# Where the top-32 mask of an attention block is made: VectorE's masked multiply, or a steep Prelu and an Exp with row sums on ScalarE

## The chip, the cores and the metric

The kernel runs on one core of a Trainium2 chip. The core has five engines, each with an instruction queue of its own that runs strictly in order: TensorE (PE, with its weight loads shown apart as PEld), VectorE (DVE), ScalarE (ACT), GpSimd (POOL) and SyncE (SP, which here only issues DMAs). They wait for each other through semaphores. The metric is the device time of one launch in microseconds (us); lower is better.

## The reference, cut to what matters

Attention that keeps the 32 largest scores of each row, followed by two feed-forward blocks.

```python
scores = scale * np.matmul(q, k.transpose(0, 1, 3, 2))     # 4 batches, 8 heads, 576 x 576, scale 1/8
kth = np.partition(scores, -32, axis=-1)[..., -32:-31]
scores = np.where(scores >= kth, scores, -1e9)
attn = np.exp(scores - max(scores)); attn /= attn.sum(-1) + 1e-9
x = attn @ v
h = x @ w_in;  g = P(h) / (Q(h) + 1e-6);  y = g @ w_out    # 2304 tokens, 512 -> 2048 -> 512
h = y @ w_in2; g = h * np.cos(h);         out = g @ w_out2
```

## The kernel before

**Attention.** A unit is 128 query rows of one pair of heads, so a tile of scores is 128 x 2 x 576 in fp32, and there are 72 units. `qk(i)` multiplies on PE into the PSUM tile `sx`, and ACT copies each head's half (j = 0, 1) into the SBUF tile `sS`. `topk(i)` is a generator of pieces. DVE takes the larger and the smaller of the two half rows into `e` (two TENSOR_TENSOR), and then finds the 32 largest in four rounds of MAX8 with MATCH_REPLACE8 between them; they end up sorted in `hd`, so `hd[0]` is the row's maximum and `hd[31]` the threshold. ACT makes `nb`, the maximum times -1/8, after the first round. After the last round ACT writes exp(score/8 + nb) for the whole row over `e`. Then, in two last pieces (one for each j), DVE reads `sS` and `e` once more: it keeps `e` where the score is at least the threshold, writes zero elsewhere, and adds up the row into `sum`. That is the SCALAR_TENSOR_TENSOR `e<-sS,hd,e`, and its row sum comes out with a DVE_READ_ACCUMULATOR. `av(i)` transposes `e` on PE (`pp`), ACT copies the transposes to SBUF (`pt`), and PE multiplies by v. `norm` divides by the row sums.

**Feed-forward blocks.** Eight units make 256 tokens, and for these the two blocks run in 8 groups each: `in1`, `mid1`, `end1`, `out1`, then `in2`, `mul2`, `out2`. Every fp32 product is three fp32r matmuls (high and low parts). ACT evacuates PSUM (`w`, `hs`) and does Abs, Ln, Exp, Sin and the affine steps; DVE and POOL do the products of two tensors.

**Weights.** In the first 16 units or so the kernel also takes 64 pieces of 64-bit weights apart into fp32 high and low parts (`conv`, tiles `raw`, `cb`), on ACT, POOL, DVE and PE, and stores low parts back to DRAM.

**Order.** The pieces of `topk` and the steps of the feed-forward blocks are laid into one list of slots, five slots to a unit. The mask pieces of unit i run in the first slot of unit i + 1, ahead of `av(i)`. From there a scheduler that follows the list and a modelled timeline settles the order on each engine's queue. `sS` and `e` have two buffers each. All ACT, DVE and POOL instructions are recorded by one helper, so they all show line L79.

Of the kernel before, what the change touches and what calls it, by code (L numbers as in the profile page):

```python
# [10 lines left out]
F32 = mybir.dt.float32  # L11
# [3 lines left out]
AF = mybir.ActivationFunctionType  # L15
ALU = mybir.AluOpType
# [7 lines left out]
P = 128  # L24
# [3 lines left out]
SCALE = 0.125  # L28
HALF = S // 2
NEG = -3.0e38  # L30
VW = 640
TWO_PI = 6.283185307179586
MAGIC = 12582912.0
# [16 lines left out]
NC0 = 36  # L50
C2 = 80
PM = 150
PMASK = range(0)
WA, PA = 12, 90
WG, PG = 10, 90
N1, NU, N2, NST, NGG = 2, 2, 3, 4, 3
# [32 lines left out]
def body(tc, out, qt, kt, vt, ident_d, w1_d, w1o_d, a_d, b_d, w2_d, w2o_d):  # L89
    nc = tc.nc  # L90
    V, A, G = Windowed(tc, nc.vector, WIN, PM), Windowed(tc, nc.scalar, WA, PA), Windowed(tc, nc.gpsimd, WG, PG)
    PE, SP = nc.tensor, nc.sync

    with ExitStack() as ctx:
        def pool(name, bufs=1, **k):
            return ctx.enter_context(tc.tile_pool(name=name, bufs=bufs, **k))
# [5 lines left out]
        sml = pool("sml", 4)  # L102
# [25 lines left out]
        sx = ps_s.tile([P, 2, 512], F32, name="sx")  # L128
# [6 lines left out]
        def store_k(x, b, pr):  # L135
            raw, hi = x[:, 0].bitcast(F32), x[:, 1]
            A.activation(hi, raw, AF.Copy)
            G.tensor_sub(raw, raw, hi.bitcast(F32))
            hi = hi.bitcast(F32)
            top, bot = slice(0, D), slice(D, P)  # L140
            d = kdr[b, pr]
            for o, i_ in ((d[top, 0], hi[top]), (d[bot, 0], raw[top]), (d[bot, 1], hi[bot]), (d[top, 1], raw[bot])):
                SP.dma_start(out=o, in_=i_)
# [36 lines left out]
        def load_v(i):  # L180
# [4 lines left out]
            for j, (b, _) in enumerate(qts[n]):  # L185
                v = kv.tile([P, VW], F32, tag="v", bufs=VB, name=f"v{i}_{b}")
                A.dma_start(out=v, in_=vt[b, pr])
# [91 lines left out]
        def halves(ap):  # L279
            return ap.rearrange("p (a c) -> p a c", a=2)  # L280

        def after(mm, bank):
            for x in order[bank]:
                tc.add_manual_dep(mm.ins, x, mybir.DependencyInfo(mybir.DependencyClass.NoSync, mybir.DependencyReason.DATA), reason="bank")

        def qk(i):
            n, pr = units[i]
            raw, hi, lo = (*qpair[i // 2], None, None)[:3]
            kvs = ins[i]
            m = P // len(kvs)  # L290
            st[i] = sb = att.tile([P, 2, S], F32, tag="sS", bufs=2, name=f"sS{i}")
            for j in range(2):
                rows = slice(j * D, (j + 1) * D)
                for c, (k, _) in reversed(list(enumerate(kvs))):
                    q0 = i % 2 * P
                    qs, qc = slice(0, (c + 1) * m), slice(q0, q0 + (c + 1) * m)
                    for hf in range(2):
                        o = sx[qs, hf, :HALF]
                        hs = slice(hf * HALF, (hf + 1) * HALF)
                        if n < 2:  # L300
                            mm = PE.matmul(o, raw[rows, j, qc], k[rows, 0, hs].bitcast(F32), start=True, stop=True)
                            after(mm, hf)
                        else:
                            mm = PE.matmul(o, hi[:, j, qc], k[:, j, hs], start=True, stop=False, skip_group_check=True)
                            after(mm, hf)
                            mm = PE.matmul(o, lo[:, j, qc], k[:, j, hs], start=False, stop=True, skip_group_check=True)
                        order[hf] = [mm.ins.name]
                A.activation(halves(sb[:, j]), sx[:, :, :HALF], AF.Copy)
            if n == 1:
                store_k(kvs[0][0], 0, pr)  # L310

        def topk(i):
            n, pr = units[i]
            sc = st.pop(i)
            tiles = [sc[:, j] for j in range(2)]
            e = att.tile([P, 2, S], F32, tag="e", bufs=EB, name=f"e{i}")
            et[i] = e
            kb, t = n // 2, n % 2
            if i % 8 == 0:
                sums[kb] = sml.tile([P, 2, H], F32, tag="sum", bufs=2, name=f"sum{kb}")  # L320
            sm = sums[kb][:, t]
            hds = sml.tile([P, 2, 32], F32, tag="hd", bufs=2, name=f"hd_{i}")
            hd = [hds[:, j] for j in range(2)]
            nb = sml.tile([P, 2], F32, tag="nb", bufs=2, name=f"nb_{i}")
            big = [e[:, j, :HALF] for j in range(2)]
            both = [e[:, j] for j in range(2)]

            def top(j, x, r):
                V.max(out=hd[j][:, 8 * r:8 * r + 8], in_=x[j])

            def drop(j, x, r):
                V.match_replace(out=x[j], in_to_replace=hd[j][:, 8 * r:8 * r + 8], in_values=x[j], imm_value=NEG)

            l, r = sc[:, :, :HALF], sc[:, :, HALF:]
            V.tensor_tensor(e[:, :, :HALF], l, r, op=ALU.max)
            top(0, big, 0)
            yield
            V.tensor_tensor(e[:, :, HALF:], l, r, op=ALU.min)
            top(1, big, 0)
            A.activation(nb, hds[:, :, 0], AF.Copy, scale=-SCALE)  # L340
            yield
            for step in (((drop, big, 0), (top, big, 1)), ((drop, big, 1), (top, both, 2)), ((drop, both, 2),)):
                for f, *x in step:
                    for j in range(2):
                        f(j, *x)
                yield
            for j, s in enumerate(tiles):
                top(j, both, 3)
                A.activation(e[:, j], s, AF.Exp, bias=nb[:, j:j + 1], scale=SCALE)
            yield  # L350
            for j, s in enumerate(tiles):
                row = sm[:, 2 * pr + j:2 * pr + j + 1]
                if i in PMASK:
                    G.tensor_scalar(s, s, hd[j][:, 31:32], 1.0, op0=ALU.is_ge, op1=ALU.mult)
                    G.tensor_mul(e[:, j], e[:, j], s)
                    A.activation(s, e[:, j], AF.Copy, accum_out=row)
                else:
                    V.scalar_tensor_tensor(e[:, j], s, hd[j][:, 31:32], e[:, j], op0=ALU.is_ge, op1=ALU.mult, accum_out=row)
                yield

        def av(i):
# [279 lines left out]
        def attention():  # L641
            load_k(1)
            load_v(0)
            qk(0)
            prev = None
            nrm, fresh, held = [], [], []
            for i in range(nu + 1):
                if LQ == 0 and i % 2 == 0 and i + 2 < nu:
                    load_q(i + 2)
                if i + 1 < nu:  # L650
                    qk(i + 1)
                if i + 2 < nu:
                    load_k(i + 2)
                for x, a in held:
                    store_k(x, *a)
                held = [(prep(*a), a) for a in preps.get(i, [])]
                t = topk(i) if i < nu else iter([None] * 9)
                for p in range(5):
                    if p == 0 and prev is not None:
# [49 lines left out]
def _layout(q, k, v, moe_w_in, moe_w_out, moe_a, moe_b, moe2_w_in, moe2_w_out):  # L709
# [9 lines left out]
    vp = v.reshape(B, NP, 2, S, D)  # L719
    vh = np.zeros((B, NP, P, VW), np.float32)  # L720
    vh[..., :512] = vp[:, :, :, :512].reshape(B, NP, 2, 4, P, D).transpose(0, 1, 4, 3, 2, 5).reshape(B, NP, P, 512)
# [19 lines left out]
```

## Time and profile before

| | |
|---|---|
| time, median of 3 runs | 1469.39 us (1466.33 to 1470.24) |
| the profiled execution | 1473.49 us, its span 1471.7 us |
| PE busy | 1270.3 us, 86% of the span |
| DVE busy | 1283.4 us, 87% |
| ACT busy | 1082.1 us, 74% |
| POOL busy | 680.4 us, 46% |
| mean granted TensorE clock | 0.92 |
| bytes moved by DMA | 314.98 MB, mean 214 GB/s |

Busy time is the time in which at least one instruction of the engine is under way. Instructions overlap a little at their ends, and matmuls a good deal, so the mean duration of one is longer than its share of the queue. The shares of the whole span mix stages: the attention pieces run from the start to about 1277 us, the weights are taken apart until about 356 us, and after 1277 us only feed-forward work is left.

### The profile page before, as it was taken

The page shows a single profiled execution, that of the slowest core. Times are in us where ns is not written, and L with a number is a line of the kernel's source. Part 1 is how long each engine was busy: PE and PEld are TensorE (multiplying, and loading weights), DVE is VectorE, ACT ScalarE, POOL GpSimd, SP SyncE. Part 2 cuts the span into 40 slices and gives each one's busy share as a digit, 9 for nine tenths or more (in the row PEclk, how much of TensorE's full clock was granted, in tenths as well). Part 3 has the DMA queues.
Part 4 walks back from the last instruction along what each step waited for, and adds up shares of the span by engine and source line. Part 5 has one row for each costly group of instructions (what it writes and reads, how often), then busy time and mean ns, then how long its engine had stood idle before and what let it go on. Part 6 is the DMA issues. An engine that isn't in the chain of part 4 may idle for free.

```text
span 1471.7 us, 25059 instructions
## 1 busy us (share of the span) xinstructions
PE 1270.3 (86%) x9016; PEld 1120.9 (76%) x9016; DVE 1283.4 (87%) x2477; ACT 1082.1 (74%) x1873; POOL 680.4 (46%) x503
## 2 busy tenths in 40 slices
PE   5766787657898799989988998999999899999988
PEld 2434565546896698889888997888899799988986
DVE  6999999789999999989989999999999999745533
ACT  5777778665787678778877877878878577876643
POOL 3879466654354346335544644444545344420000
PEclk9677798757999899999999999999999999999999
DMA  7886756775456656555765665565467677656677
GB/s 227 286 280 209 238 183 201 239 229 197 136 190 200 208 183 211 190 175 205 241 221 176 219 212 190 182 215 198 176 219 247 215 253 260 226 196 226 233 239 230
DMA packets 141549, 314.98 MB, mean 214 GB/s; under 512 B 12016, under 2 KB 28528, under 8 KB 141424
## 3 DMA queue, kind: packets, MB, share of 16 engines
q1 hardware_dynamic: 122832, 261.99, 53.4%
q10 hardware_dynamic: 18592, 51.39, 10.4%
q8 instruction: 71, 1.16, 0.3%
q14 instruction: 54, 0.44, 0.1%
HBM read 278.20 MB, written 35.13 MB: 213 GB/s over the span
## 4 chain that ended last, share of the span: by engine, by line
DVE 37%; PE 28%; ACT 13%; DMA 11%; issue 6%; POOL 5%; SPq 0%; ACTq 0%; POOLq 0%; DVEq 0%
DVE e L79 17%; DVE hd L79 8%; PE o L558 6%; DVE u L79 5%; PE h L444 4%; PE h L446 4%; PE h L445 4%; DVE cb L79 2%; POOL cb L79 2%; PE y L503 2%; PE y L502 2%; ACT L79 2%; DMA raw<-w 2%; DMA w1ol<-w1ol 2%; PE y L501 2%
## 5 line engine op out<-in xcount | busy, mean ns | idle before, releaser
L79 DVE MAX8 hd<-e 128x8 f32<-128x288 f32 (+1 forms) x576 | 322.3, 592 | 0.0
L558 PE MATMUL o<-w2o,gg 128*128 128x512 f32 x864 | 233.8, 409 | 9.7 <-DMA w2o<-w2o 8.5
L79 DVE MATCH_REPLACE8 e<-hd,e 128x288 f32<-128x288 f32 (+1 forms) x432 | 230.2, 537 | 0.0
L558 PEld LDWEIGHTS o<-w2o,gg 128*128 128x128 f32 x864 | 160.6, 197 | 40.5 <-DMA w2o<-w2o 9.9
L79 DVE TENSOR_TENSOR e<-sS 128x576 f32<-128x576 f32 x144 | 166.9, 1196 | 24.9 <-ACT sS L79 15.2
L444 PE MATMUL h<-xh,w1hi 128*128 128x256 f32 x576 | 171.6, 298 | 12.5 <-ACT hs L79 6.3
L502 PE MATMUL y<-gg,w1o 128*128 128x256 f32 x576 | 169.3, 294 | 6.7 <-POOL gg L79 6.6
L445 PE MATMUL h<-xl,w1hi 128*128 128x256 f32 x576 | 167.6, 291 | 6.8 <-DVE xl L79 6.8
L501 PE MATMUL y<-gg,w1o 128*128 128x256 f32 x576 | 169.2, 294 | 4.6 <-ACT gg L79 4.6
L79 POOL TENSOR_TENSOR gg<-u,gg 128x512 fp32r<-128x512 f32 x64 | 91.8, 1435 | 174.5 <-ACT gg L79 158.8
L444 PE MATMUL h<-x2h,w2hi 128*128 128x256 f32 x576 | 165.9, 288 | 5.2 <-ACT w L79 2.7
L503 PE MATMUL y<-gg,w1ol 128*128 128x256 f32 x576 | 167.8, 291 | 1.6 <-DMA w1ol<-w1ol 1.5
L446 PE MATMUL h<-x2h,lo 128*128 128x256 f32 x576 | 164.9, 286 | 3.2 <-DMA lo<-w2lo 3.2
L446 PE MATMUL h<-xh,lo 128*128 128x256 f32 x576 | 166.4, 289 | 0.0
L445 PE MATMUL h<-x2l,w2hi 128*128 128x256 f32 x576 | 164.5, 286 | 2.1 <-DVE x2l L79 2.1
L79 DVE SCALAR_TENSOR_TENSOR e<-sS,hd,e 128x576 f32<-128x576 f32 x144 | 151.7, 1068 | 16.4 <-ACT e L79 16.2
L79 POOL TENSOR_TENSOR u<-u,w 128x512 f32<-128x512 f32 x64 | 91.8, 1435 | 157.3 <-ACT u L79 148.9
L79 POOL TENSOR_TENSOR rr<-rr,hs 128x512 f32<-128x512 f32 x56 | 78.2, 1418 | 127.7 <-ACT rr L79 127.7
L79 ACT ACTIVATE e<-sS,nb 128x576 f32<-128x576 f32 x144 | 107.9, 772 | 29.8 <-DVE hd L79 29.5
L444 PEld LDWEIGHTS h<-xh,w1hi 128*128 128x128 f32 x576 | 113.4, 197 | 18.1 <-ACT hs L79 8.4
L502 PEld LDWEIGHTS y<-gg,w1o 128*128 128x128 f32 x576 | 113.9, 198 | 10.9 <-POOL gg L79 9.0
L501 PEld LDWEIGHTS y<-gg,w1o 128*128 128x128 f32 x576 | 114.3, 198 | 9.1 <-ACT gg L79 7.5
(1167 smaller groups left out, 3793.1 us busy)
## 6 DMA issues: line engine op xcount, KB each, us to landing
w2o<-w2o SPq DMA_DIRECT2D x144, 512.0 KB, 4.2
lo<-w1lo SPq DMA_DIRECT2D x72, 512.0 KB, 4.0
w1ol<-w1ol SPq DMA_DIRECT2D x72, 512.0 KB, 3.8
lo<-w2lo SPq DMA_DIRECT2D x72, 512.0 KB, 4.4
k<-kdr ACTq DMA_DIRECT2D x44, 576.0 KB, 5.0
raw<-w SPq DMA_DIRECT2D x32, 512.0 KB, 4.6
v<-vt ACTq DMA_DIRECT2D x48, 320.0 KB, 3.7
qr<-qt ACTq DMA_DIRECT2D x36, 256.0 KB, 4.0
```

The source lines that it names most:

```text
L79: r = f(*a, **k)
L444: PE.matmul(h[:, i, :], wh, xh[:, c, :], start=(c == 0), stop=False)
L445: PE.matmul(h[:, i, :], wh, xl[:, c, :], start=False, stop=False)
L446: PE.matmul(h[:, i, :], lo[:, i, c, :], xh[:, c, :], start=False, stop=(c == NCC - 1))
L501: PE.matmul(y[:, c, :], w1o[:, f, cs], gh[:, i, :], start=(f == 0 and c % 2 == 0), stop=False, skip_group_check=True)
L502: PE.matmul(y[:, c, :], w1o[:, f, cs], gl[:, i, :], start=False, stop=False, skip_group_check=True)
L503: PE.matmul(y[:, c, :], wl[:, i, cs], gh[:, i, :], start=False, stop=(f == NF - 1), skip_group_check=True)
L558: PE.matmul(o[:, t, :], l[:, i, ts], wt[i][:, r], start=(f == 0 and r == 0 and l is gh), stop=(f == NF - 1 and l is gl), skip_group_check= ...
```

## The change

The scores are scaled by 1/8 as they leave PSUM. After the last MAX8, ACT makes `nt` = -threshold for both heads. For each head it writes Prelu(score - threshold) over `e`, with slope 1 above zero and 2^120 below, then makes `nb` = threshold - maximum with an Identity, and then writes Exp(e + nb) in place, with the row sum in the same instruction. What lies under the threshold has become hugely negative, so its exponential is zero. The mask pass on DVE is gone, and with it the early `nb`.

```diff
+STEEP = 2.0 ** 120
...
-                A.activation(halves(sb[:, j]), sx[:, :, :HALF], AF.Copy)
+                A.activation(halves(sb[:, j]), sx[:, :, :HALF], AF.Copy, scale=SCALE)
...
             nb = sml.tile([P, 2], F32, tag="nb", bufs=2, name=f"nb_{i}")
+            nt = sml.tile([P, 2], F32, tag="nt", bufs=2, name=f"nt_{i}")
...
             top(1, big, 0)
-            A.activation(nb, hds[:, :, 0], AF.Copy, scale=-SCALE)
             yield
...
-            for j, s in enumerate(tiles):
+            for j in range(2):
                 top(j, both, 3)
-                A.activation(e[:, j], s, AF.Exp, bias=nb[:, j:j + 1], scale=SCALE)
             yield
-            for j, s in enumerate(tiles):
-                row = sm[:, 2 * pr + j:2 * pr + j + 1]
...
-                    V.scalar_tensor_tensor(e[:, j], s, hd[j][:, 31:32], e[:, j], op0=ALU.is_ge, op1=ALU.mult, accum_out=row)
+            for j in range(2):
+                if j == 0:
+                    A.activation(nt, hds[:, :, 31], AF.Copy, scale=-1.0)
+                A.activation(e[:, j], sc[:, j], AF.Prelu, bias=nt[:, j:j + 1], alpha=STEEP)
+                A.activation(nb[:, j:j + 1], hd[j][:, 0:1], AF.Identity, scale=-1.0, bias=hd[j][:, 31:32])
+                A.activation(e[:, j], e[:, j], AF.Exp, bias=nb[:, j:j + 1], accum_out=sm[:, 2 * pr + j:2 * pr + j + 1])
                 yield
```

ACT's queue before, between two evacuations of unit 36's transposes, with the exponentials of unit 37 (`e37`; `h`, `w`, `r`, `rr`, `n`, `gg`, `ob` belong to the feed-forward blocks):

```order
L79 ACTIVATE pt36a_6564<-pp36a_6559 128x512
L79 ACTIVATE sS38_6537<-sx_94 128x576
L79 ACTIVATE e37_6549<-sS37_6326,nb_37_6551 128x576 x2
L79 ACTIVATE hs2_2_6703<-h1_2_2_6677 128x512
L79 ACTIVATE r3_4_6623<-q3_4_6622,qc_114 128x512
L79 ACTIVATE rr2_2_6702<-hs2_2_6703,quarter_110 128x512
L79 ACTIVATE pt36b_6571<-pp36b_6566 128x512
```

Both exponentials of unit 37 stand side by side, right behind an evacuation of scores. ACT's queue now, at the same place:

```order
L79 ACTIVATE pt36a_6675<-pp36a_6670 128x512
L79 ACTIVATE n2_2_6816<-rr2_2_6813,magic_112 128x512
L79 ACTIVATE nb_37_6660<-hd_37_6659 128x1
L79 ACTIVATE nt_37_6661<-hd_37_6659 128x2
L79 ACTIVATE nb_37_6660<-hd_37_6659 128x1
L79 ACTIVATE e37_6658<-sS37_6429,nt_37_6661 128x576 x2
L79 ACTIVATE w3_5_6938<-h0_3_5_6913 128x512
L79 ACTIVATE e37_6658,sum4_5631<-e37_6658,nb_37_6660 128x576
L79 ACTIVATE ob1_0_6836<-o1_5408 128x512
L79 ACTIVATE sS38_6643<-sx_94 128x576
L79 ACTIVATE gg1_3_4_6983<-u3_4_6735 128x512
L79 ACTIVATE e37_6658,sum4_5631<-e37_6658,nb_37_6660 128x576
```

The three small instructions and both Prelus stand where the two exponentials stood; the exponentials follow with other work between them. In both programs the whole ACT queue holds 67 ACT_TABLE_LOADs.

DVE's queue before, from unit 37's last rounds to unit 38's first:

```order
L79 MATCH_REPLACE e37_6549<-hd_37_6550,e37_6549 128x576 x2
L79 MAX hd_37_6550<-e37_6549 128x8 x2
L79 SCALAR_TENSOR_TENSOR u3_4_6624<-u3_4_6624,nega_108,w3_4_6621 128x512
L79 SCALAR_TENSOR_TENSOR e37_6549,sum4_5537<-sS37_6326,hd_37_6550,e37_6549 128x576 x2
L79 SCALAR_TENSOR_TENSOR q3_4_6622<-q3_4_6622,r3_4_6623 128x512
L79 SCALAR_TENSOR_TENSOR u3_4_6624<-u3_4_6624,nega_108,r3_4_6623 128x512
L79 SCALAR_TENSOR_TENSOR rr2_2_6702<-n2_2_6705,rr2_2_6702 128x512
L79 SCALAR_TENSOR_TENSOR u3_4_6624<-q3_4_6622,u3_4_6624 128x512
L79 TENSOR_TENSOR e38_6749<-sS38_6537 128x2x288 x2
```

The masks of unit 37 (`e37_6549,sum4_5537`) stand between steps of `end1`. DVE's queue now, at the same place:

```order
L79 MATCH_REPLACE e37_6658<-hd_37_6659,e37_6658 128x576 x2
L79 MAX hd_37_6659<-e37_6658 128x8 x2
L79 SCALAR_TENSOR_TENSOR q3_4_6733<-q3_4_6733,r3_4_6734 128x512
L79 SCALAR_TENSOR_TENSOR u3_4_6735<-u3_4_6735,nega_108,r3_4_6734 128x512
L79 SCALAR_TENSOR_TENSOR rr2_2_6813<-n2_2_6816,rr2_2_6813 128x512
L79 SCALAR_TENSOR_TENSOR u3_4_6735<-q3_4_6733,u3_4_6735 128x512
L79 TENSOR_TENSOR e38_6861<-sS38_6643 128x2x288 x2
```

The two mask instructions, which waited for ACT's exponentials, are gone from between the last MAX8 and the next unit.

## Rows read from the trace of the kernel before

**Rows 1.** Busy time of each engine by stage: us, busy (instructions), clock, DMA, GB/s

```profile
core 0: us, PE busy (x) PEld busy (x) DVE busy (x) ACT busy (x) POOL busy (x), PEclk, DMA share, GB/s
...
29.00:166.00 137.00, 92.97 (x353) 54.97 (x354) 133.88 (x254) 100.62 (x194) 108.16 (x87) 0.69 0.78 255
166.00:356.00 190.00, 131.03 (x745) 105.74 (x744) 169.92 (x289) 131.95 (x242) 111.57 (x88) 0.76 0.68 219
356.00:485.00 129.00, 108.97 (x854) 99.56 (x851) 125.90 (x261) 96.95 (x169) 61.09 (x42) 0.97 0.54 176
485.00:1161.00 676.00, 630.29 (x4832) 583.30 (x4832) 642.09 (x1299) 533.33 (x925) 325.43 (x225) 0.97 0.60 204
1161.00:1277.00 116.00, 113.41 (x981) 106.96 (x983) 109.01 (x212) 89.32 (x153) 48.44 (x35) 0.97 0.70 242
1277.00:1471.70 194.70, 179.71 (x1239) 163.81 (x1235) 87.34 (x136) 114.19 (x165) 16.52 (x13) 0.99 0.68 225
```

**Rows 2.** The page's chain that ended last: its share of the span by engine

```profile
DVE 37%; PE 28%; ACT 13%; DMA 11%; issue 6%; POOL 5%; SPq 0%; ACTq 0%; POOLq 0%; DVEq 0%
```

**Rows 3.** Groups of the whole run: count, busy us, mean ns, idle before and releaser

```profile
L79 DVE SCALAR_TENSOR_TENSOR e<-sS,hd,e 128x576 f32<-128x576 f32 x144 | 151.7, 1068 | 16.4 <-ACT e L79 16.2
L79 DVE DVE_READ_ACCUMULATOR e<-sS,hd,e 128x1 f32 x144 | 11.1, 77 | 0.0
L79 ACT ACT_TABLE_LOAD x67 | 86.0, 1283 | 3.4 <-issue 2.1
```

**Rows 4.** The mask pass in two stretches, 29 to 166 us, then 485 to 1161 us

```profile
L79 DVE SCALAR_TENSOR_TENSOR e<-sS,hd,e 128x576 f32<-128x576 f32 x17 | 22.6, 1333 | 1.2 <-ACT e L79 1.2
...
L79 DVE SCALAR_TENSOR_TENSOR e<-sS,hd,e 128x576 f32<-128x576 f32 x81 | 79.8, 1004 | 9.5 <-ACT e L79 9.3
```

**Rows 5.** ACT's groups from 485 to 1161 us

```profile
L79 ACT ACTIVATE e<-sS,nb 128x576 f32<-128x576 f32 x80 | 59.5, 771 | 14.1 <-DVE hd L79 14.0
...
L79 ACT ACTIVATE n<-rr,magic 128x512 f32<-128x512 f32 x40 | 28.7, 717 | 1.2 <-DMA out<-ob 0.8
L79 ACT ACTIVATE r<-w 128x512 f32<-128x512 f32 x40 | 25.2, 630 | 1.5 <-POOL gg L79 1.0
...
L79 ACT ACTIVATE nb<-hd 128x2 f32<-128x2 f32 x40 | 8.1, 201 | 28.3 <-DVE hd L79 28.0
```

**Rows 6.** ACT's timeline at four places: start us, duration us, instruction

```profile
685.00 0.20 ACT L79 ACTIVATE nb<-hd 128x2 f32<-128x2 f32 x1 [1.48 <-DVE hd L79]
685.11 0.71 ACT L79 ACTIVATE n<-rr,magic 128x512 f32<-128x512 f32 x1
...
695.09 1.45 ACT L79 ACTIVATE e<-sS,nb 128x576 f32<-128x576 f32 x2
696.43 0.60 ACT L79 ACTIVATE hs<-h 128x512 f32<-128x512 f32 x1
...
697.52 0.72 ACT L79 ACTIVATE rr<-hs,quarter 128x512 f32<-128x512 f32 x1
698.14 0.60 ACT L79 ACTIVATE pt36b<-pp36b 128x512 f32<-128x512 f32 x1
...
1302.62 0.71 ACT L79 ACTIVATE rr<-hs,quarter 128x512 f32<-128x512 f32 x1
1303.37 0.72 ACT L79 ACTIVATE n<-rr,magic 128x512 f32<-128x512 f32 x1
```

**Rows 7.** Waits of ACT, then of DVE, 485 to 1161 us: total, times, longest

```profile
ACT nb L79 <- DVE hd L79: 28.0, 24, 2.6
...
ACT e L79 <- DVE hd L79: 14.0, 15, 2.5
...
DVE e L79 <- ACT e L79: 9.3, 7, 2.5
```

**Rows 8.** Waits of all engines, 166 to 356 us: total, times, longest

```profile
ACT raw L79 <- DMA raw<-w2o: 12.3, 9, 4.3
...
PE pp13a L374 <- DVE e L79: 9.1, 1, 9.1
```

More of the change, by code (lines that the diff above doesn't have):

```diff
@@ L52 @@
 PM = 150
-PMASK = range(0)
 WA, PA = 12, 90
@@ L314, in topk @@
             sc = st.pop(i)
-            tiles = [sc[:, j] for j in range(2)]
             e = att.tile([P, 2, S], F32, tag="e", bufs=EB, name=f"e{i}")
@@ L346, in topk @@
                 yield
-            for j, s in enumerate(tiles):
+            for j in range(2):
                 top(j, both, 3)
-                A.activation(e[:, j], s, AF.Exp, bias=nb[:, j:j + 1], scale=SCALE)
             yield
-            for j, s in enumerate(tiles):
-                row = sm[:, 2 * pr + j:2 * pr + j + 1]
[L353 to L357, printed above, removed]
-                    V.scalar_tensor_tensor(e[:, j], s, hd[j][:, 31:32], e[:, j], op0=ALU.is_ge, op1=ALU.mult, accum_out=row)
+            for j in range(2):
[4 more added lines that the diff above has]
+                A.activation(e[:, j], e[:, j], AF.Exp, bias=nb[:, j:j + 1], accum_out=sm[:, 2 * pr + j:2 * pr + j + 1])
                 yield
```

## The prediction

> **What bounds the kernel now.** I read busy time by stage first, because the shares of the whole span mix stages with different limits [rows 1]. I cut at the first transposes of units 0, 8, 16, 24, 64 and 71. Eight units take 137 us, then 190, then 129; the forty units from 485 to 1161 us take 676, about 135 for eight; the last seven take 116; and 194.7 us of feed-forward work are left when the attention pieces are over. The reader is to see which engine is fullest in each. DVE is busy 133.88 of 137 us, 169.92 of 190, 125.90 of 129 and 642.09 of 676: 98, 89, 98 and 95%. From 1161 us on it is PE, 113.41 of 116 (98%). PE stands close behind DVE in the long stretch too, 630.29 of 676 (93%), but matmuls overlap, so this count holds the time in which a matmul drains while nothing follows it. ACT has 533.33 of 676 (79%). Then the chain of waits: DVE has 37% of it, PE 28%, ACT 13%, DMA 11% [rows 2]. So DVE leads until 1161 us, but not alone. Work that leaves DVE is worth something until then, and nothing after.
>
> **The change part by part.**
>
> *Removed from DVE.* 144 mask passes, 151.7 us in all, 1068 ns each; the 144 reads of the accumulator (77 ns) lie inside the start of the next instruction [rows 3]. An instruction overlaps its neighbour by about 0.07 us, so some 1.0 us of queue goes with each, 2.0 us per unit. By stage: 22.6 us from 29 to 166 us, where one pass takes 1333 ns, and 79.8 us from 485 to 1161 us [rows 4]; in the two stages between, 16 passes of 1.0 us each. DVE's wait for ACT's exponential ahead of the mask goes too, 9.3 us in the long stretch [rows 7].
>
> *Added to ACT.* Per unit, two Prelus over 576 elements and one small instruction for each head; `nt` takes the place of the old `nb`, the same shape, at no change. The trace has no Prelu; the nearest row is the exponential, the same tile with the same kind of bias operand, 771 ns alone [rows 5], and two of them hold the queue for 1.34 us before the next starts [rows 6]. So 0.67 us each. The small `nb` now takes a bias from memory: the old one holds the queue 0.11 us [rows 6], and a bias operand adds 717 - 630 = 87 ns, by two operations of one shape with and without it [rows 5]. So 0.20 us each. The row sum out of the exponential has no row on ACT. From below it costs nothing, as DVE's read does; from above, as much as a small instruction, 0.20 us. I take 0.08, DVE's duration, which is the nearest row. Last, an instruction that reads what the one right ahead of it wrote: Identity to Identity starts 0.75 us after when it depends and 0.62 when it doesn't [rows 6], so 0.13 us. The order above puts other work between most of them; I take one per unit. The sum is 2 x 0.67 + 2 x 0.20 + 2 x 0.08 + 0.13 = 2.0 us per unit. The ends are 2 x 0.67 + 2 x 0.11 = 1.6, and 2 x 0.77 + 2 x 0.30 + 2 x 0.20 + 4 x 0.13 = 3.1 us.
>
> *Is a pass on ACT dearer than on DVE?* Over the same 128 x 576 fp32 the exponential takes 771 ns and the mask 1068 [rows 3, 5]. The Trainium skill, ScalarE: Activation LUTs, Rules for kernel authors, says the opposite: simple steps such as relu, max and mul belong on VectorE, which it puts at up to about three times faster per element in bf16. By that rule a Prelu would cost ACT more than the 1068 ns that DVE gives up; the trace shows the reverse for this fp32 pass.
>
> *Moved and free.* The scale on the copy out of PSUM replaces a constant; nothing is added. The new program holds as many table loads as the trace of before, 67 at 1283 ns [rows 3], so Prelu brings no switch. The early `nb` had ACT wait 28.0 us for the first MAX8 in the long stretch, and the exponential another 14.0 for the last [rows 7]; now there is one such wait, on the last MAX8. Behind it on ACT's queue stand an evacuation of `h` and one of scores, and PE and DVE wait for these, as they did behind the exponential. `e` now comes from ACT, at the end of a row of dependent instructions, instead of from DVE. The order leaves several ACT instructions between the second exponential and the first evacuated transpose that needs it, so I cost this at nothing; if that cover goes, PE waits by its transposes. The worst such wait of before is 9.1 us, once [rows 8]. The 8 x 2.0 us per group of units on DVE and the same on ACT nearly cancel; what counts is that DVE was at 95 to 98% and ACT at 79.
>
> **The sum by stage.** I allow the fullest engine 95%, what DVE holds in the long stretch.
> - 29 to 166 us: DVE falls to 112, ACT rises to 100.6 + 16 = 117, POOL has 108. 117 / 0.95 = 123; with three engines so near each other I take 126: **-11**.
> - 166 to 356 us: DVE 153, ACT 148, PE 131 at a granted clock of 0.76. DVE's 20 us of idle time are where the weights' DMAs set the pace (ACT waits 12.3 us for `raw` [rows 8]). If all of the removed work counts it is -18, if the DMAs hold it 0; I take half: **-9**.
> - 356 to 485 us: DVE 110, ACT 113, PE 109. 113 / 0.95 = 119: **-9**.
> - 485 to 1161 us: DVE 642 - 75 = 567, ACT 533 + 81 = 614, PE 630. ACT at 95% gives 646, PE at the 98% that it reaches after 1161 us gives 643. I take 650: **-26**.
> - 1161 to 1277 us: PE is at 98% already: **-1**. After that nothing changes.
>
> That is -56, so the profiled execution would go from 1473.5 to about 1418. It stood 4.1 us above the median of 1469.4; taken off, **1414 us**.
>
> **The rivals.**
> - *PE and the handoffs hold the long stretch.* PE's 93%, and its 28% of the chain, speak for it; that DVE has the larger share of the chain speaks against. Then only the first three stages gain, 29 us: **1440 us**.
> - *ACT takes DVE's place, and it is slower.* At 3.1 us per unit ACT gets 533 + 124 = 657 in the long stretch; at 95% that is 692, 16 us more than now. The first and third stages give 132 and 128 (-5 and -1), the last one of the attention +1. Sum +11: **1480 us**. The point from which it decides is 0.95 x 676 - 533 = 109 us on forty units, 2.7 us per unit. For it: the row sum's price is unknown, and every evacuation that PE needs stands in the same queue. Against: four of its prices would all have to be at their upper ends.
> - *More than I take.* With 1.6 us per unit ACT has 597 in the long stretch, 628 at 95% (-48), PE's count shrinks as its waits do, and the three stages before it give their full -18, -18 and -13: -97, **1372 us**. PE's 630 speaks against it.
> - *The wait only moves.* ACT waits for the last MAX8 and everyone behind it waits along, as much as DVE saves: **1468 us**. The waits that go, 28.0 and 9.3 us, speak against.
>
> **How the numbers follow.** My forecast 0.50, with a range of its own of 1390 to 1432; PE holds it 0.20; more 0.10; no change 0.06; slower 0.14. A measurement of this kernel can't tell less than about 0.3%, some 4 us, from no change. So faster 0.80, same 0.06, slower 0.14. The range leaves out the slower case and half of the case with more, and takes in no change: 1372 to 1468.
>
> **What would show it right or wrong.** In the profile after, no SCALAR_TENSOR_TENSOR on `e`, and DVE's busy time near 1135 us; ACT's near 1082 + 145 = 1227; Prelu near 0.77 us; the stage of forty units at about 650 us with ACT at 95%. If ACT's groups on `e` and `nb` add up to over 2.7 us per unit more than before, the slower case is on. If DVE falls and the long stretch keeps its 676 us, PE's waits will say who holds it: waits for `w`, `hs` or `pt` from ACT mean the queue there, none mean PE itself. I would be wrong at the root if the transposes of `e` waited on ACT in every unit.

## The result: 1.2% slower, and the profile after

The changed kernel takes 1485.86 us (median of four runs, 1484.74 to 1494.18) against 1467.89 us before (four runs); the ratio is 1.0116, with a 95% interval of 1.0079 to 1.0153. The forecast was 1414 us, faster. The profiled execution after is 1494.18 us, its span 1492.4 us; it is the longest of the four, 8.3 us above their median, so its stages are a little long.

The first part of the page of the changed kernel, busy time over the whole run:

```profile
PE 1274.8 (85%) x9016; PEld 1122.6 (75%) x9016; DVE 1145.2 (77%) x2189; ACT 1200.6 (80%) x2305; POOL 667.5 (45%) x503
```

DVE has lost 138 us (1283.4 before; 148 were forecast) and ACT gained 118.5 (1082.1 before; 145 were forecast). The time went the other way all the same. Busy time by stage, cut at the same units as [rows 1] (us; busy time and count of each engine, granted clock, share of DMA, GB/s):

```profile
27.00:165.00 138.00, 92.35 (x355) 54.17 (x353) 117.91 (x221) 115.30 (x245) 105.31 (x88) 0.70 0.80 257
165.00:347.00 182.00, 122.41 (x699) 97.66 (x699) 148.04 (x250) 139.74 (x282) 106.08 (x86) 0.77 0.67 217
347.00:485.00 138.00, 118.75 (x896) 109.00 (x895) 122.55 (x240) 114.02 (x227) 62.28 (x43) 0.94 0.54 174
485.00:1184.00 699.00, 641.61 (x4855) 591.05 (x4856) 565.59 (x1136) 602.41 (x1167) 320.23 (x225) 0.96 0.60 198
1184.00:1304.00 120.00, 116.69 (x1026) 109.49 (x1025) 89.41 (x180) 102.40 (x197) 51.03 (x37) 1.00 0.73 247
1304.00:1492.40 188.40, 169.99 (x1170) 154.71 (x1168) 87.44 (x137) 110.34 (x163) 14.43 (x11) 0.98 0.69 221
```

The long stretch of forty units has gone from 676 to 699 us, and in it no engine is full any more: DVE is at 81%, ACT at 86%, and PE's count at 92%, below its 93% of before. The first and third stages have not gained either (137 to 138, 129 to 138); the second has (190 to 182), and so has the feed-forward work at the end, which the change does not touch (194.7 to 188.4). PE's own busy time in the long stretch is 11.3 us more than before (630.29 to 641.61), at a mean granted clock of 0.96 instead of 0.97.

The new instructions on ACT, in its groups of the whole run (count, busy us, mean ns, idle us before, releaser):

```profile
L79 ACT ACTIVATE e<-e,nb 128x576 f32<-128x576 f32 x144 | 110.5, 770 | 0.2
L79 ACT ACTIVATE e<-sS,nt 128x576 f32<-128x576 f32 x144 | 103.5, 767 | 0.0
...
L79 ACT ACTIVATE nb<-hd 128x1 f32<-128x1 f32 x144 | 41.3, 288 | 22.6 <-DVE hd L79 22.5
...
L79 ACT ACTIVATION_READ_ACCUMULATOR e<-e,nb 128x1 f32 x144 | 28.0, 195 | 0.0
```

The places where other engines stand idle, in the page's groups, of the changed kernel first and then of the kernel before:

```profile
L79 DVE TENSOR_TENSOR e<-sS 128x576 f32<-128x576 f32 x144 | 159.7, 1148 | 124.8 <-ACT sS L79 71.5
...
L440 PE MATMUL h<-xh,w1hi 128*128 128x256 f32 x576 | 173.7, 302 | 23.0 <-ACT hs L79 10.0
...
L497 PE MATMUL y<-gg,w1o 128*128 128x256 f32 x576 | 169.8, 295 | 13.9 <-ACT gg L79 13.9
L440 PE MATMUL h<-x2h,w2hi 128*128 128x256 f32 x576 | 167.4, 291 | 10.8 <-ACT w L79 9.9
```

```profile
L79 DVE TENSOR_TENSOR e<-sS 128x576 f32<-128x576 f32 x144 | 166.9, 1196 | 24.9 <-ACT sS L79 15.2
L444 PE MATMUL h<-xh,w1hi 128*128 128x256 f32 x576 | 171.6, 298 | 12.5 <-ACT hs L79 6.3
...
L501 PE MATMUL y<-gg,w1o 128*128 128x256 f32 x576 | 169.2, 294 | 4.6 <-ACT gg L79 4.6
...
L444 PE MATMUL h<-x2h,w2hi 128*128 128x256 f32 x576 | 165.9, 288 | 5.2 <-ACT w L79 2.7
```

The first DVE instruction of a unit, the TENSOR_TENSOR on the scores, had 24.9 us of idle time ahead of it before and has 124.8 now, 71.5 of it for ACT's copy of the scores out of PSUM. Not all of this is the work of the new instructions: `x1_no_mask` below, which takes the mask off DVE and adds nothing to ACT, already has 86.3 us there, and is fast.

```profile
L79 DVE TENSOR_TENSOR e<-sS 128x576 f32<-128x576 f32 x144 | 170.8, 1225 | 86.3 <-ACT sS L79 36.2
```

So much of the new idle time is DVE's freed time, and the wait for the copy is what ACT's new work lengthens (36.2 to 71.5 us). PE's idle time says more of the time lost. Ahead of the three groups shown it rises from 12.5, 4.6 and 5.2 us to 23.0, 13.9 and 10.8, for ACT in the main. Added up over the whole run, PE's waits for ACT rise from 105 us to 160 and its waits for DVE fall from 50 to 7.

One unit shows how DVE comes to wait, first on ACT, then on DVE, then PE's last matmul on the scores that ACT copies at 729.96 (start us, duration us):

```profile
724.03 0.63 ACT L79 ACTIVATE sS<-sx 128x576 f32<-128x576 f32 x1
724.57 0.28 ACT L79 ACTIVATE nb<-hd 128x1 f32<-128x1 f32 x1
...
725.93 0.19 ACT L79 ACTIVATE nt<-hd 128x2 f32<-128x2 f32 x1
726.03 0.28 ACT L79 ACTIVATE nb<-hd 128x1 f32<-128x1 f32 x1
726.22 0.62 ACT L79 ACTIVATE gg<-rr 128x512 fp32r<-128x512 f32 x1
726.74 1.43 ACT L79 ACTIVATE e<-sS,nt 128x576 f32<-128x576 f32 x2
...
729.20 0.77 ACT L79 ACTIVATE e<-e,nb 128x576 f32<-128x576 f32 x1
729.87 0.19 ACT L79 ACTIVATION_READ_ACCUMULATOR e<-e,nb 128x1 f32 x1
729.96 0.64 ACT L79 ACTIVATE sS<-sx 128x576 f32<-128x576 f32 x1
```

```profile
722.16 1.41 DVE L79 MAX8 hd<-e 128x8 f32<-128x576 f32 x2
725.63 0.75 DVE L79 SCALAR_TENSOR_TENSOR u<-u,nega,w 128x512 f32<-128x512 f32 x1 [2.07 <-POOL u L79]
730.63 1.43 DVE L79 TENSOR_TENSOR e<-sS 128x576 f32<-128x576 f32 x2 [4.24 <-ACT sS L79]
```

```profile
726.00 0.29 PE L306 MATMUL sx<-k,ql 128*128 128x288 f32 x1
```

DVE is done with unit 38's last MAX8 at 723.6 us. ACT copies out the first head's scores of unit 39 at 724.03 us. PE has the second head's ready at 726.3 us, but ACT first works off the small instructions, both Prelus and one exponential with its accumulator read, with feed-forward work between them; only behind these, at 729.96 us, does it copy out the second head's scores, and DVE, with nothing of the mask left to do, waits 4.24 us for them.

### The profile page after: what moved, and what is told of

It is laid out like the page before. It is cut to its first block, busy times and chain, and to the rows that moved or that the text cites. A ratio compares the mean times of both kernels' runs of the same rounds, so it can differ in the third digit from the quotient of the medians.

```text
span 1492.4 us, 25201 instructions
## 1 busy us (share of the span) xinstructions
PE 1274.8 (85%) x9016; PEld 1122.6 (75%) x9016; DVE 1145.2 (77%) x2189; ACT 1200.6 (80%) x2305; POOL 667.5 (45%) x503
## 3 DMA queue, kind: packets, MB, share of 16 engines
q10 hardware_dynamic: 18592, 51.39, 10.6%
## 4 chain that ended last, share of the span: by engine, by line
PE 24%; DVE 24%; ACT 21%; DMA 8%; issue 4%; POOL 2%; ACTq 0%; SPq 0%; POOLq 0%; DVEq 0%
DVE e L79 9%; DVE hd L79 6%; PE o L554 5%; DVE u L79 5%; ACT e L79 5%; PE h L440 4%; PE h L442 3%; PE h L441 3%; ACT L79 3%; DMA w2o<-w2o 2%; ACT gg L79 2%; ACT sS L79 2%; ACT r L79 2%; DVE q L79 2%; PE sx L388 1%
## 5 line engine op out<-in xcount | busy, mean ns | idle before, releaser
L79 DVE TENSOR_TENSOR e<-sS 128x576 f32<-128x576 f32 x144 | 159.7, 1148 | 124.8 <-ACT sS L79 71.5
L554 PE MATMUL o<-w2o,gg 128*128 128x512 f32 x864 | 225.9, 399 | 9.3 <-DMA w2o<-w2o 8.0
L554 PEld LDWEIGHTS o<-w2o,gg 128*128 128x128 f32 x864 | 154.6, 190 | 39.0 <-DMA w2o<-w2o 9.0
L497 PE MATMUL y<-gg,w1o 128*128 128x256 f32 x576 | 169.8, 295 | 13.9 <-ACT gg L79 13.9
L440 PE MATMUL h<-x2h,w2hi 128*128 128x256 f32 x576 | 167.4, 291 | 10.8 <-ACT w L79 9.9
L79 POOL TENSOR_TENSOR rr<-rr,hs 128x512 f32<-128x512 f32 x56 | 75.5, 1371 | 134.7 <-ACT rr L79 124.8
L440 PEld LDWEIGHTS h<-x2h,w2hi 128*128 128x128 f32 x576 | 111.4, 193 | 15.6 <-ACT w L79 13.2
L441 PEld LDWEIGHTS h<-xl,w1hi 128*128 128x128 f32 x576 | 115.5, 201 | 4.4 <-DVE xl L79 3.2
```

The source lines that it names most:

```text
L79: r = f(*a, **k)
L440: PE.matmul(h[:, i, :], wh, xh[:, c, :], start=(c == 0), stop=False)
L441: PE.matmul(h[:, i, :], wh, xl[:, c, :], start=False, stop=False)
L497: PE.matmul(y[:, c, :], w1o[:, f, cs], gh[:, i, :], start=(f == 0 and c % 2 == 0), stop=False, skip_group_check=True)
L554: PE.matmul(o[:, t, :], l[:, i, ts], wt[i][:, r], start=(f == 0 and r == 0 and l is gh), stop=(f == NF - 1 and l is gl), skip_group_check= ...
```

## The experiments

Three theories were to be told apart. **Q**: it is the added time on ACT's queue that costs, because the copies out of PSUM and the steps that PE and DVE wait for stand behind it. **L**: it is the longer way from the last MAX8 to the transposes. **P**: PE and the handoffs hold the kernel anyway, so freeing DVE is worth little. Every ratio is against the kernel before on the same chip, with its 95% interval; gains and losses against it in us are taken from the ratios. Every version is put in order anew by the scheduler, so an edit can also change the order of work that it does not name.

**Only the removal** (`x1_no_mask`).

```diff
-                    V.scalar_tensor_tensor(e[:, j], s, hd[j][:, 31:32], e[:, j], op0=ALU.is_ge, op1=ALU.mult, accum_out=row)
...
+                G.memset(sums[kb], 576.0)
```

> The kernel before with the mask pass on VectorE left out and nothing put in its place (the exponentials go unmasked and the row sums are a constant, so the output is not the attention's). Theory Q, ScalarE's queue: in the changed kernel the gain of the freed VectorE is there and the added ScalarE work eats it; then this run shows the gain alone, some 50 us, 1410 to 1425 us. Theory P, TensorE and the handoffs between the engines: freeing VectorE is worth little in itself; then 1450 us or more.

Measured: 1428.05 us, 0.9722 [0.9686, 0.9757], a gain of some 41 us. That is 3 us above Q's range and 22 below P's; but the long stretch shows P's part. The stage is 661 us there, 15 less than before, with DVE at 86%:

```profile
462.00:1123.00 661.00, 625.57 (x4835) 580.09 (x4834) 571.55 (x1137) 534.90 (x927) 317.60 (x229) 0.98 0.63 209
```

70 us of DVE work gone from a stage whose fullest engine was DVE gave 15. The rest of the gain came from what lay before 485 us, some 23 us, and a few from 1161 to 1277 us. It is not the price of DVE's time alone: `e` is also ready earlier, and PE's waits for `e` ahead of the transposes, added up, fall from 33 us to 8.5.

**Only the addition** (`x2_both`): the changed chain on ACT, with slope 1, and DVE's mask pass kept behind it.

```diff
-                A.activation(e[:, j], sc[:, j], AF.Prelu, bias=nt[:, j:j + 1], alpha=STEEP)
+                A.activation(e[:, j], sc[:, j], AF.Prelu, bias=nt[:, j:j + 1], alpha=1.0)
...
+                V.scalar_tensor_tensor(e[:, j], sc[:, j], hd[j][:, 31:32], e[:, j], op0=ALU.is_ge, op1=ALU.mult, accum_out=row)
```

> The changed kernel's whole chain on ScalarE (with a slope of 1, so that nothing is masked by it), and the mask pass kept on VectorE as before: the added ScalarE work alone. Theory Q: some 60 to 90 us slower than the kernel before, 1530 to 1560 us. Theory P: the added work is mostly hidden, and the time is near that of the changed kernel, 1480 to 1500 us.

Measured: 1564.43 us, 1.0666 [1.0618, 1.0713]: 98 us slower, above even Q's figure. Here DVE's mask also waits for the longer chain: its idle time ahead of the mask rises from 16.4 us [rows 3] to 40.2. The addition is dear. How much of the 98 us is ACT's time and how much the longer way to the mask, this run does not say.

**The addition with nobody waiting for it** (`x6_detached`): on `x1_no_mask`, the same ACT work over scores that are no longer read, and half of that (`x13_detached_half`, for one head of two).

```diff
+                A.activation(sc[:, j], sc[:, j], AF.Prelu, bias=zero[:, 0:1], alpha=STEEP, accum_out=zs[:, 2:3])
+                A.activation(zs[:, j:j + 1], zero[:, 0:1], AF.Identity, scale=-1.0, bias=zero[:, 0:1])
```

> The kernel with the mask pass left out (x1_no_mask), and on ScalarE the same added work as in the changed kernel (two Prelus over 576 elements with a row sum, two small Identities per unit), but written over scores that nothing reads any more, so that no result hangs on it. The output is not the attention's. Theory Q, the queue: it is the added time on ScalarE's queue that costs, wherever it stands, because the evacuations that TensorE waits for stand behind it; 1475 to 1500 us. Theory L, the longer way from the last MAX8 to the transposes: without a reader the work costs little; 1428 to 1440 us.

> As x6_detached, with the added ScalarE work for one head of each unit instead of two, so half the dose on the kernel without the mask pass. Its output is not the attention's. Theory Q with an even price: halfway, 1446 to 1454 us. If ScalarE's time costs nothing until its queue is fuller: 1428 to 1440 us, and most of the price is in the second half. If any such work upsets the order and the amount matters little: 1460 us or more.

Measured: the whole dose 1472.41 us, 1.0014 [0.9991, 1.0037], 3 us below Q's range; the half 1448.68 us, 0.9844 [0.9801, 0.9887], inside it. From nothing to half to whole the time goes 1428, 1449, 1472. ACT's busy time goes along, in the first part of the three pages, `x1_no_mask` first, then half and whole:

```profile
PE 1258.5 (88%) x9016; PEld 1117.0 (78%) x9016; DVE 1137.7 (80%) x2189; ACT 1079.1 (75%) x1873; POOL 663.8 (46%) x512
```

```profile
PE 1260.4 (87%) x9016; PEld 1112.7 (77%) x9016; DVE 1132.9 (78%) x2189; ACT 1142.2 (79%) x2089; POOL 659.7 (45%) x513
```

```profile
PE 1272.8 (87%) x9016; PEld 1122.9 (77%) x9016; DVE 1142.3 (78%) x2189; ACT 1202.3 (82%) x2305; POOL 665.2 (45%) x513
```

123 us of ACT time that nothing depends on cost 44 us, 0.36 us each, on an engine that is at 75 to 82%; evenly, as far as the half's interval of 6 us to either side can tell. That is Q, and it gives back all of the removal's 41 us. With L alone it would have cost little, and if any disturbance of the order did it, the half would have cost as much as the whole. PE shows it in the same place as in the changed kernel. This is PE's group on the first matmul of `h` in the long stretch, `x1_no_mask` first, then `x6_detached`:

```profile
L438 PE MATMUL h<-x2h,w2hi 128*128 128x256 f32 x320 | 92.3, 288 | 1.1 <-ACT w L79 1.0
```

```profile
L444 PE MATMUL h<-x2h,w2hi 128*128 128x256 f32 x320 | 94.3, 295 | 8.3 <-ACT w L80 8.3
```

`h` has one PSUM buffer, so the next group's matmuls wait until ACT has copied out the last one's result, and that copy stands in the same queue as the added work. In the long stretch, which goes from 661 to 694 us, PE's waits for ACT add up to 10.9 us in `x1_no_mask` and to 28.9 in `x6_detached`; another 10 us are PE's own busy time (625.57 to 635.87), whose rise was not looked into.

**What is left for L.** The changed kernel is some 15 us above `x6_detached` (1.0116 against 1.0014). PE's waits for `e` ahead of the transposes are not the place: they add up to 10.6 us in the changed kernel, 9.3 in `x6_detached` and 33 before. Its waits for ACT's copies of the transposes (`pt`) in the long stretch are 21.0 us against 2.9, but 14.6 before; so this is a candidate and no more. `x9_late_nb` was meant to take one part alone: in the kernel before, `nb` is written behind the last MAX8.

```diff
-            A.activation(nb, hds[:, :, 0], AF.Copy, scale=-SCALE)
             yield
...
+            A.activation(nb, hds[:, :, 0], AF.Copy, scale=-SCALE)
             for j, s in enumerate(tiles):
```

> The kernel before with its small instruction on the row maximum moved behind the last MAX8, as the change has it: one part of the change alone. ScalarE's 28 us of waits for the first MAX8 in the long stretch go. Both theories: no difference that counts, 1463 to 1472 us; more would mean that ScalarE's waits there held others.

Measured: 1476.14 us, 1.0044 [1.0025, 1.0064], slower by some 6 us, where no difference was expected. It does not test what it was meant to, for `nb` did not move: the scheduler put it back behind the first round, where its input is ready, before the last round in all units. One unit, from DVE's and ACT's timelines in order of time (first round, `nb`, last round of the first head, its exponential):

```profile
702.44 0.81 DVE L79 MAX8 hd<-e 128x8 f32<-128x288 f32 x2
...
704.66 0.20 ACT L79 ACTIVATE nb<-hd 128x2 f32<-128x2 f32 x1
...
709.40 0.75 DVE L79 MAX8 hd<-e 128x8 f32<-128x576 f32 x1
...
710.46 0.77 ACT L79 ACTIVATE e<-sS,nb 128x576 f32<-128x576 f32 x1
```

So ACT's wait at `nb` is in the long stretch what it was, 29.1 us against 28.0 [rows 7], and the 6 us come with a new order of the same instructions. They say nothing for L, but they are a measure of what the order alone can do here. `x7_early` tried to shorten the way, without the small Identities (as `x3_no_nb` below) and with the Prelus and exponentials written right behind the last MAX8:

```diff
             for j in range(2):
                 top(j, both, 3)
+            A.activation(nt, hds[:, :, 31], AF.Copy, scale=-1.0)
+            for j in range(2):
+                A.activation(e[:, j], sc[:, j], AF.Prelu, bias=nt[:, j:j + 1], alpha=STEEP)
...
             yield
```

> The changed kernel without the small Identities (x3_no_nb), its Prelus and exponentials written right behind the last MAX8 in the program instead of a slot later. Theory L: the masked tile is there earlier, 5 to 15 us faster than x3_no_nb, some 1470 to 1479 us. Theory Q: the same work on the same queue, within 5 us of it, 1479 to 1489 us.

Measured: 1483.85 us, 1.0108 [1.0062, 1.0154]; no change against `x3_no_nb` (1484.14 us). The scheduler sets ACT's instructions nearly where they stood, so this says little about L. What the 15 us are for stays open.

**Less of the addition.** `x3_no_nb` drops the two small Identities (its edit is below); `x8_no_accum` leaves out the row sums as well, with a constant in their place.

```diff
-                A.activation(nb[:, j:j + 1], hd[j][:, 0:1], AF.Identity, scale=-1.0, bias=hd[j][:, 31:32])
-                A.activation(e[:, j], e[:, j], AF.Exp, bias=nb[:, j:j + 1], accum_out=sm[:, 2 * pr + j:2 * pr + j + 1])
+                A.activation(e[:, j], e[:, j], AF.Exp, accum_out=sm[:, 2 * pr + j:2 * pr + j + 1])
```

> The changed kernel without the two small Identities of a unit (the exponential is taken relative to the threshold instead of the maximum, which the division by the row sum cancels). It takes 144 x 0.29 = 41 us of busy time off ScalarE. Theory Q: 20 to 30 us faster than the changed kernel, 1455 to 1466 us. Theory P: within 8 us of it.

> The changed kernel without the small Identities and without the row sums (a constant divides, so the output is not the attention's): 144 reads of ScalarE's accumulator at 195 ns, 28 us, are gone as well. Theory Q, by the price of ScalarE time between x1_no_mask and the changed kernel (58 us of time for some 121 us of work), 10 to 15 us faster than x3_no_nb: 1469 to 1474 us. Theory L: 0 to 5 us, 1479 to 1484 us.

Measured: `x3_no_nb` 1484.14 us, 1.0116 [1.0072, 1.0160]; `x8_no_accum` 1474.83 us, 1.0043 [1.0024, 1.0063]. Against Q the first is a miss: ACT's busy time falls by 34.5 us, to 1166.1, and by the price of 0.36 that is 12 us, but the time doesn't move, as theory P had it. Its interval, 0.4% to either side, almost reaches that far, and the new order can shift as much by itself (6 us in `x9_late_nb`). Which of the two it was is open. The second is about 10 us faster than the first, near Q's figure, but for only 14.4 us less of busy time (1151.7), since each read overlaps its neighbours. Set against `x1_no_mask`, the price of 0.36 would put `x3_no_nb` at 1459 us and `x8_no_accum` at 1454; they take 25 and 21 us more. So what the changed kernel's chain costs beyond ACT's time is not smaller when ACT has less to do. The price of 0.36 is a mean over the detached work, not one that holds for each instruction.

**Giving work back.** `x5_half` masks one head on DVE and one on ACT, without the Identities. `x10_rr_dve` is `x3_no_nb` with an affine step of the second block on DVE for all tokens, `x11_half_rr` the same on `x5_half`, and `x12_rr_q_dve` is `x10_rr_dve` with a step of the first block on DVE as well.

```diff
-            if k >= DV2:
+            if k >= 0:
                 V.tensor_scalar(rr, hs, 1.0 / TWO_PI, 0.25, op0=ALU.mult, op1=ALU.add)
...
-            A.activation(q, r, AF.Identity, scale=b1, bias=b0)
+            V.tensor_scalar(q, r, b1, b0, op0=ALU.mult, op1=ALU.add)
```

> One head of each unit is masked on VectorE as before, the other by Prelu on ScalarE, both without the small Identity: half of the work moved. Theory Q: both engines below what they have at either end, 1440 to 1460 us. Theory P: between the two kernels, 1465 to 1480 us.

> The changed kernel without the small Identities (x3_no_nb), and one affine step of the second block, rr = hs/2pi + 1/4, on VectorE for all tokens instead of the last two eighths: 56 ScalarE instructions of 0.72 us, 40 us, become VectorE ones of some 0.43 us, 24 us. Theory Q (a us of ScalarE time costs about 0.36 us of time by x1_no_mask and x6_detached, a us of VectorE time about 0.27 by x1_no_mask): -14 + 6, so 8 us faster than x3_no_nb, about 1476 us. If ScalarE's queue is not what holds TensorE: no faster than 1483 us.

> The half version (x5_half) with the same affine step on VectorE. Theory Q by the same prices: -14 + 6, about 1455 us. If both engines are slack enough by now: the same as x5_half, 1459 to 1466 us.

> As x10_rr_dve, and the affine step of the first block, q = |b0| + |b1| r, on VectorE too: 72 more ScalarE instructions of 0.81 us, 58 us, become VectorE ones of some 0.43 us, 31 us. ScalarE and VectorE both have less to do than in the kernel before. Theory Q by the same prices: -35 + 15 against x3_no_nb, about 1464 us or less. If what counts is the longer way through the engines (one more handoff in the first block's chain): 1476 us or more.

Measured: `x5_half` 1462.84 us, 0.9956 [0.9935, 0.9977]; of the versions that leave out no part of the attention it is the only one clearly below the kernel before, by some 6 us. `x10_rr_dve` 1468.28 us, 0.9983 [0.9961, 1.0005]: 16 us less than `x3_no_nb` (20 by the ratios), twice what the prices said. `x12_rr_q_dve` 1473.64 us, 1.0022 [1.0001, 1.0043], where 1464 or less was expected. `x11_half_rr` 1489.72 us, 1.0139 [1.0109, 1.0168], 27 us slower than `x5_half`, where 7 faster was expected. The last two are against Q as a sum of prices. `x12_rr_q_dve` has no more to do on ACT than the kernel before (1085.4 us against 1082.1), less on DVE (1207.9 against 1283.4), and is no faster:

```profile
PE 1273.4 (86%) x9016; PEld 1119.1 (76%) x9016; DVE 1207.9 (82%) x2317; ACT 1085.4 (74%) x2033; POOL 669.5 (45%) x503
```

A step that moves to another engine adds handoffs: `rr` now goes from ACT to DVE and back. ACT's longest wait of the whole run (total us, times, longest) is in `x11_half_rr` one whose input DVE now makes, and in `x12_rr_q_dve` the same, `x11_half_rr` first:

```profile
ACT n L79 <- DVE rr L79: 48.0, 37, 4.4
```

```profile
ACT n L79 <- DVE rr L79: 49.1, 38, 3.3
```

It was 6.2 us before, and is 37.0 in `x10_rr_dve`, which gained. So this wait does not tell the version that lost 27 us from the one that won 16, and what `x11_half_rr` loses by is not shown.

## Why the prediction was wrong

- **What bounds the kernel.** DVE was the fullest engine, and the forecast took that for the bound of the first four stages. `x1_no_mask` puts a number on it: 146 us of DVE busy time gone, with the shorter way to `e` that comes with it, gives 41 us, 0.28 each. The chain of waits had hinted at it: DVE 37%, PE 28% [rows 2], no engine with most of it. The Trainium skill, Perfetto Trace Analysis, Identifying the Most-Contended Engine, says that the engine with the highest occupancy is to be optimized first. The trace agrees that DVE is that engine (87%) and `x1_no_mask` that relieving it gains, by those 41 us.
- **Removed from DVE.** 144 passes at 1.0 us went, as forecast: 138 us less, to 1145.2 us (1135 forecast).
- **Added to ACT.** 2.0 us per unit were forecast between 1.6 and 3.1; the long stretch has (602.41 - 533.33) / 40 = 1.73 us of busy time more per unit. Prelu is 767 ns, as the exponential; the small `nb` holds the queue for 0.19 us (726.03 to 726.22 in the timeline of the unit above, where feed-forward work follows it), 0.20 forecast; the accumulator read for 0.09 us (729.87 to 729.96), 0.08 forecast. No table load was added. (The 0.13 us for an instruction that reads what the one ahead of it wrote is set against a pair that is not two Identities: behind `rr` at 697.52 comes the copy `pt36b`, so the two pairs differ in more than the dependence.) This step was right: 1.73 lies inside its range, near the lower end.
- **The sum by stage** is the step that failed. (It also has a slip of 1 us: from 129 to 119 us is 10, not 9.) It gave each stage the fullest engine's busy time over 0.95, so work on an engine that isn't the fullest was free. In the long stretch ACT was to go from 79 to 95% and the stage to 650 us. It went to 699, with ACT at 86%. `x6_detached` and `x13_detached_half` show what stands in its place: ACT's time has a price well before the engine is full, 0.36 us per us, since on its queue stand the copies for which PE and DVE wait. At 0.36 for ACT's 118.5 us and 0.28 for DVE's 138 us the change comes to +43 - 39 = +4 us, which takes away the whole forecast gain; the measured +17 leaves some 13 us, whose cause stays open. A new order of the queues is a rival for part of them: it moved `x9_late_nb` by 6.
- **"I cost this at nothing"**, of the longer way to `e`: at the transposes this held, since PE's waits for `e` there fell from 33 us to 10.6, and the sign of being wrong at the root did not show. DVE's waits on ACT's mask went as forecast too. What had no price is the step beside it: the forecast had named an evacuation of `h` and one of scores behind the chain on ACT's queue, and that PE and DVE wait for these. DVE's wait for the scores' copy rose from 15.2 to 71.5 us (36.2 with the removal alone), and PE's waits for ACT from 105 to 160.
- **The rivals.** The slower one had the engine and the time nearly right, 1480 us against 1485.86. But its condition was wrong: it was to decide from 2.7 us per unit, at which ACT would be full, and the changed kernel is slower at 1.73, with ACT at 86%; so its time is near by luck. "PE and the handoffs hold the long stretch" was right of the removal in part (15 us there instead of 26, `x1_no_mask`). "The wait only moves" named ACT's wait for the last MAX8; that is not what was seen, since in the long stretch ACT's waits for it are 9.4 us at `nb` and 3.6 at `nt` now, where its waits at `nb` and `e` were 28.0 and 14.0 [rows 7].

## What to carry to other kernels

Where three in-order engines hand work to each other, time on one of them can have a price well below full use; measure it by work on its queue that nothing reads, and by leaving work out, before moving work between engines. A change that moves work from a fuller engine to a less full one is worth, to a first estimate, the difference of two such prices, here 0.28 and 0.36 us per us, and not the difference of the busy shares. The estimate is rough: in this kernel it missed by 13 to 25 us where the work moved stood in a chain of dependent steps, and a version that only changed the order moved by 6. Look also into the trace of each experiment for whether the instruction is where the edit meant it to be: in `x9_late_nb` it was not. Ask also who stands behind the moved instructions on their new queue: here it was the copy out of PSUM with which the next unit starts.

## What the runs showed of the hardware

A row sum out of an ACT instruction comes as an instruction of its own, ACTIVATION_READ_ACCUMULATOR, 195 ns, against 77 ns for DVE's [rows 3]; the next ACT instruction starts some 0.09 us after it starts (729.87 to 729.96 above). An ACT instruction on one element per partition with a bias from memory takes 288 ns, against 201 for two elements with constants [rows 5]. Prelu over 128 x 576 takes as long as the exponential, 767 and 770 ns.
